# Scores and AV on 64-key partition halves, with the global outputs merged into AV

## The chip, the cores and the metric

One core of one Trainium2 chip. The metric is the device time in microseconds (us) of one execution. The engines are named as in the profile: PE (matmul), PEld (PE's weight loads, which overlap its matmuls), DVE (vector), ACT (activation), POOL and SP. Every run told here was in the fast state, except the one single-round run whose state is unknown, which is marked.

## The reference

Attention with a band of local keys and 32 global tokens, then a two-layer MLP with a quick GELU:

```python
batch, n_heads, seq_l, seq_g, head_dim = (8, 8, 512, 32, 64)
window = 32
k_all = concatenate([k_g, k_l]); v_all = concatenate([v_g, v_l])
out_g = softmax(scale * q_g @ k_all.T) @ v_all               # global queries see all keys
s_ll  = scale * q_l @ k_l.T, masked to |pos - pos'| <= window # local: band of 65 keys
s_lg  = scale * q_l @ k_g.T                                   # ... and the 32 global keys
out_l = softmax([s_lg, s_ll]) @ [v_g, v_l]
x = [out_g, out_l] as tokens x 512
h = x @ w_in                        # 512 -> 2048
g = h / (1 + exp(-1.702 * h))
out = g @ w_out                     # 2048 -> 512
```

## The kernel before

It works on head groups of four heads (two per batch element, 16 in all) and on MLP blocks of 512 tokens. While the MLP's second product of one block runs, the attention of the next block is fitted between its matmuls. All of these parts are matmuls on PE:

- `S`, the scores: transposed, keys on the output partitions. A round has two chunks of 128 keys; each chunk meets only the queries that its band touches. A 32-row part of PE holds one head, so four heads run at once on 32x128 tiles.
- `K` and `ekU`: scores of the global keys, and the opening of the three accumulators (sums and two halves of the output) with the global values.
- `U`, AV: adds exp(scores) times values, and times ones for the sums, into those accumulators; 128x32 tiles, four heads at once.
- `Gm`: the outputs of the global queries, 66 columns each.

```python
WIN = ((0, 10), (6, 12), (14, 12), (22, 10))      # per chunk: first query residue, how many
qt = consts.tile([128, 24, 32], F32)              # queries, with global queries before and after
...
def S(self, rnd, ...):
    for c in (2 * rnd, 2 * rnd + 1):
        ...
        for e in range(2):                        # the two halves of a head's dimension
            for j in range(4):                    # four heads, four 32-row tiles
                nc.tensor.matmul(ps[j][:, off : off + n],
                    lhsT=self.k[p, 128 * c : 128 * c + 128, e],
                    rhs=self.q[p, lo:hi, r0 : r0 + nr, e], ...)
...
def U(self, unit):                                # unit 0: sums, 1 and 2: output halves
    for c in range(4):
        ...
        for j in range(4):
            lv = (ones32 if unit == 0 else self.v[:, j, c, :D] ...)
            nc.tensor.matmul(ov[32 * j : 32 * j + 32, :] ... [:, :, r0 : r0 + nr],
                lhsT=lv, rhs=self.E[c // 2][:, j, at : at + 16 * nr],
                start=False, stop=(c == 3), ...)

def Gm(self, og=None):
    for c in range(5):                            # 4 key chunks and the global keys
        for j in range(4):
            ...
            nc.tensor.matmul(og[32 * j : 32 * j + 32, : D + 2], lhsT=lv, rhs=rv, ...)
...
def phase_o(i):                                   # second MLP product of block i
    ...                                           # with the attention of block i + 1
    o(0)                                          # o(t): 16 matmuls of 512 columns
    c.S(0)
    a.UG(c)                                       # ekUs, then U for three units, then Gm
    ...
    o(1)
    c.S(1)
    ...
    o(2)
    a2.S(0)
    c.UG(a2)
    ...
    o(3)
```

## Time and profile before

| kernel before | |
|---|---|
| time, median of 3 runs | 311.04 us (310.78 to 311.09) |
| span of the profiled run | 309.3 us |
| PE busy | 97% |
| steady period, one MLP block | 34.40 us (first MLP matmul of block 3 at 125.89, of block 4 at 160.29) |
| longest weight-load wait in AV that no semaphore explains | 0.4 us |

How to read it: the page's slices are fortieths of the span, each digit a busy share in tenths. PE is full everywhere, so the path that sets the end is PE itself, and an instruction or a pause added to PE is paid in full. The prediction shows these lines. One line of the waits view is added here, because the result turns on it. It gives the engine, the line that waited, what it waited for ("issue": nothing that the profile shows), then us in total, times, and the longest in us:

```profile
PEld L397 <- issue: 7.3, 20, 0.4
```

L397 is the matmul of `U`. Its weight loads paused 20 times with no semaphore to blame, never over 0.4 us: ordinary pauses while PE was busy with the matmuls ahead.

### The profile page before, as it was taken

To read this page: it belongs to the slowest core of one execution; us is meant where nothing else is said; L and a number is where in the kernel's file an instruction comes from. 1 tells how busy PE (TensorE), PEld (TensorE's weight loads), DVE (VectorE), ACT (ScalarE), POOL (GpSimd) and SP (SyncE) were. 2 spreads that over 40 slices of the span, in tenths; PEclk is the share of its full clock that TensorE was granted. 3 is DMA by queue.
4 is the path that set the end of the run, shared out by engine and by line. 5 is a ranking of instruction groups with operands and counts; after the bars stand their busy time and mean duration, and the time that the engine had idled before them with its cause. 6 is when DMAs were issued, how large, how long until landed. Compare 5 with 4: busy or idle time off the path is not lost.

```text
span 309.3 us, 7765 instructions
## 1 busy us (share of the span) xinstructions
PE 299.2 (97%) x3230; PEld 149.3 (48%) x3265; DVE 211.0 (68%) x446; ACT 167.6 (54%) x251; POOL 54.1 (18%) x86
## 2 busy tenths in 40 slices
PE   7899999999999999999999999999999999999994
PEld 6544445444454455444454455445454454446653
DVE  6668857978957876776867876776777855573320
ACT  4728475475546735565556645565456651673421
POOL 8542754630050001400050002100000000000000
PEclk9999999999999999999999999999999999999999
DMA  7999999999289013951199013901120012201122
GB/s 193 176 209 206 201 138 217 213 184 100 61 79 192 5 36 72 131 107 30 45 95 173 8 37 71 101 0 36 36 61 10 2 44 46 51 0 35 35 68 69
DMA packets 53859, 27.60 MB, mean 89 GB/s; under 512 B 42432, under 2 KB 43712, under 8 KB 53824
## 3 DMA queue, kind: packets, MB, share of 16 engines
q0 software_dynamic: 45696, 16.95, 48.2%
q1 hardware_dynamic: 7648, 9.51, 12.6%
q10 hardware_dynamic: 480, 0.66, 0.7%
q8 instruction: 25, 0.41, 0.6%
q14 instruction: 10, 0.08, 0.1%
HBM read 35.13 MB, written 8.91 MB: 142 GB/s over the span
## 4 chain that ended last, share of the span: by engine, by line
PE 88%; DVE 4%; ACT 2%; DMA 2%; issue 1%; POOL 1%; ACTq 0%; POOLq 0%
PE op L491 35%; PE hp L466 35%; PE s L297 6%; PE ov L397 4%; PE ov L374 3%; DMA rk<-in_k_l_dram 2%; ACT e L327 1%; DVE xL L430 1%; PE s L316 1%; PE op L503 1%; DVE gT L474 1%; PE s L466 1%; PE s L415 1%; ACT th L473 1%; PE kb L316 1%
## 5 line engine op out<-in xcount | busy, mean ns | idle before, releaser
L491 PE MATMUL op<-w_out_sb,gT 128*128 128x512 bf16 x504 | 120.0, 380 | 1.7 <-issue 0.5
L474 DVE SCALAR_TENSOR_TENSOR gT<-th,hp 128x512 bf16<-128x512 f32 (+1 forms) x140 | 91.1, 656 | 41.8 <-ACT th L473 40.5
L466 PE MATMUL hp<-xL,w_in_sb 128*128 128x512 bf16 x487 | 108.4, 379 | 0.7
L473 ACT ACTIVATE th<-hp 128x512 f32<-128x512 f32 (+1 forms) x140 | 79.8, 573 | 42.9 <-PE hp L466 39.4
L466 PEld LDWEIGHTS <-w_in_sb 128*128 128x128 bf16 x576 | 56.1, 98 | 65.0 <-issue 1.3
L491 PEld LDWEIGHTS <-gT 128*128 128x128 bf16 x528 | 49.3, 98 | 56.4 <-issue 3.5
L327 ACT ACTIVATE e<-s 128x1712 bf16<-128x1712 f32 x31 | 49.5, 1597 | 15.8 <-PE s L415 8.9
L505 ACT ACTIVATE ob<-op 128x512 f32<-128x512 f32 (+2 forms) x35 | 20.5, 585 | 60.3 <-PE op L491 57.7
L89 POOL DMA_DIRECT2D v<-in_v_l_dram x24 | 18.7, 786 | 115.9 <-PE s L415 111.0
L421 DVE STREAM_TRANSPOSE sT<-ov 128x512 f32<-128x512 f32 x15 | 10.8, 717 | 29.1 <-PE ov L397 29.1
L334 DVE TENSOR_TENSOR e<-e,mask 128x1408 bf16<-128x1408 bf16 x28 | 24.4, 871 | 6.5 <-ACT e L327 6.5
L297 PE MATMUL s<-q,kT 32*128 32x228 bf16 (+5 forms) x528 | 21.1, 280 | 0.9 <-DVE q L259 0.7
L430 DVE TENSOR_TENSOR xL<-ov,rs 128x512 bf16<-128x512 f32 x30 | 19.4, 686 | 1.8 <-PE ov L397 0.5
L297 PEld LDWEIGHTS <-kT 32*128 32x128 bf16 x528 | 11.1, 95 | 14.8 <-issue 9.4
L255 DVE STREAM_TRANSPOSE kT<-rk 128x512 f32<-128x512 f32 (+1 forms) x17 | 16.9, 993 | 1.4 <-DMA rk<-in_k_l_dram 1.3
L362 ACT ACTIVATE ek<-kb 128x512 bf16<-128x512 f32 x16 | 9.6, 601 | 9.5 <-PE kb L316 9.5
L397 PE MATMUL ov<-e,v 128*32 128x160 bf16 (+1 forms) x480 | 12.1, 239 | 0.0
L425 DVE STREAM_TRANSPOSE rs<-rT 128x512 f32<-128x512 f32 x16 | 11.4, 711 | 0.5
L259 DVE STREAM_TRANSPOSE q<-rq 128x512 f32<-128x512 f32 (+1 forms) x17 | 10.7, 634 | 0.0
L397 PEld LDWEIGHTS <-v 128*32 128x32 bf16 x512 | 10.0, 97 | 0.9 <-issue 0.9
L316 PE MATMUL kb<-q,kgT 32*32 32x512 bf16 x128 | 10.0, 386 | 0.0
L466 PE MATMUL hp<-xG,w_in_sb 128*128 128x256 bf16 x64 | 9.6, 273 | 0.1
(78 smaller groups left out, 165.9 us busy)
## 6 DMA issues: line engine op xcount, KB each, us to landing
out_dram<-ob SPq DMA_DIRECT2D x132, 64.0 KB, 1.7
v<-in_v_l_dram POOLq DMA_DIRECT2D x32, 128.0 KB, 6.5
rq<-in_q_l_dram POOLq DMA_DIRECT2D x6, 512.0 KB, 8.5
rk<-in_k_l_dram POOLq DMA_DIRECT2D x6, 512.0 KB, 10.4
w_out_sb<-in_moe_w_out_dram POOLq DMA_DIRECT2D x4, 512.0 KB, 11.3
w_in_sb<-in_moe_w_in_dram POOLq DMA_DIRECT2D x4, 256.0 KB, 10.2
w_in_sb<-in_moe_w_in_dram POOLq DMA_DIRECT2D x2, 512.0 KB, 12.5
rq<-in_q_l_dram POOLq DMA_DIRECT2D x3, 256.0 KB, 7.9
```

Of the source, the lines that this page charges most:

```text
L89: nc.gpsimd.dma_start(out=vtiles[b % 2][p, s, :, :, :D], in_=vf[b, g][:, hs])
L255: nc.vector.transpose(self.kT.rearrange("p (r t) -> p t r", t=16)[:, lo:hi], loaded[self.b][0][:, self.u].bitcast(F32)[:, 32 * lo : 32 * hi])
L297: nc.tensor.matmul(ps[j][:, off : off + n], lhsT=self.k[p, 128 * c : 128 * c + 128, e], rhs=self.q[p, lo:hi, r0 : r0 + nr, e], start=(e == ...
L327: nc.scalar.activation(e[:, :, :RW], self.ps[:, :, :RW], AF.Exp, scale=scale)
L334: nc.vector.tensor_mul(e, e, mask[:, rnd : rnd + 1, :].to_broadcast([128, 4, LW]))
L397: nc.tensor.matmul(ov[32 * j : 32 * j + 32, :].rearrange("p (t r) -> p t r", t=16)[:, :, r0 : r0 + nr], lhsT=lv, rhs=self.E[c // 2][:, j, ...
L430: nc.vector.tensor_mul(self.x[:, 2 * self.u + h, :], self.st[1 + h], self.st["rs"])
L466: nc.tensor.matmul(hp[:, : width(i)], lhsT=w_in_c[:, fc // 8, kc, fc % 8 // 2, :, fc % 2], rhs=(xL[i] if i < B else xG)[:, kc, :], start=( ...
L473: nc.scalar.activation(th[:, :n], hp[:, :n], AF.Tanh, scale=0.851)
L474: nc.vector.scalar_tensor_tensor(gTs[i][:, fc, :n], in0=th[:, :n], scalar=1.0, in1=hp[:, :n], op0=ALU.add, op1=ALU.mult)
L491: nc.tensor.matmul(op, lhsT=gTs[i][:, fc, tci * 128 : tci * 128 + 128], rhs=w_out_sb[:, fc, :], start=(first and fc == 4 * f4), stop=(fc = ...
L505: nc.scalar.activation(ob[:, lo:hi], op[:, lo:hi], AF.Copy, scale=0.5)
```

## The change

Its intent is to stream fewer columns. A half chunk of 64 keys with a band of 32 on each side meets 128 queries, so splitting the 128-key chunks trims what is computed outside the band; on 64x32 tiles the two halves run at the same time. The 66-column global outputs become a fourth unit beside the three of AV, so that every phase has two units, one on each row half. A PE drain (meant to hold the next matmuls back until those before it are done) is put between the second and the third phase, where the units change row halves, so that the two halves do not write one accumulator in the wrong order.

```diff
-    WIN = ((0, 10), (6, 12), (14, 12), (22, 10))
-        qt = consts.tile([128, 24, 32], F32, name="q%d" % i)
+        qt = consts.tile([128, 24, 36], F32, name="q%d" % i)
...
         def S(...)
-            for c in (2 * rnd, 2 * rnd + 1):
+            for ci in range(2):
+                c = 2 * rnd + ci
                 for e in range(2):
-                    for j in range(4):
-                        nc.tensor.matmul(ps[j][:, off : off + n],
-                            lhsT=self.k[p, 128 * c : 128 * c + 128, e],
-                            rhs=self.q[p, lo:hi, r0 : r0 + nr, e], ...)
+                    for h in range(2):
+                        r0 = 4 * (2 * c + h)
+                        for j in range(4):
+                            nc.tensor.matmul(ps[j][64 * h : 64 * h + 64, off : off + 8 * (hi - lo)],
+                                lhsT=self.k[p, k, e], rhs=self.q[p, lo:hi, r0 : r0 + 8, e], ...)
...
-        def U(self, unit): ...
-        def Gm(self, og=None): ...
+        def L(self, og=None):
+            for units in ((0, 2), (1, 3), (2, 0), (3, 1)):      # one unit per row half
+                if units == (2, 0):
+                    nc.tensor.drain()
+                for c in range(5 if 3 in units else 4):
+                    for j in range(4):
+                        for h, unit in enumerate(units):
+                            p = slice(64 * h, 64 * h + 64)
+                            ...
+                            else:
+                                nc.tensor.matmul(self.st[unit][o] ... [:, :, lo:hi], lhsT=lv,
+                                    rhs=e[:, 32 - 32 * h : 160 - 32 * h] ..., ...)
...
-    (prologue: a.U, c.B, c.S, a.Gm and the first MLP products interleaved; v_g by way of SP and a cast)
+    (prologue: all of a.L, then c's scores, then all of c.L, then the MLP; v_g straight to bf16 by POOL)
...
-            (last head group: units between output matmuls)
+            (last head group: ekUs and L, as everywhere)
```

The last two hunks are told in words; many lines are cut.

> **What bounds the kernel now.** I read the page first (engines, slices), then the groups of PE by shape, then the chain of waits, then the timeline of PE in one steady stretch. The page:
>
> ```profile
> span 309.3 us, 7765 instructions
> PE 299.2 (97%) x3230; PEld 149.3 (48%) x3265; DVE 211.0 (68%) x446; ACT 167.6 (54%) x251; POOL 54.1 (18%) x86
> PE   7899999999999999999999999999999999999994
> PEclk9999999999999999999999999999999999999999
> DMA  7999999999289013951199013901120012201122
> q8 instruction: 25, 0.41, 0.6%
> ```
>
> PE is busy in every slice at full clock. DVE (68%) and ACT (54%) have room; DMA is only dense in the first tenth. So the time is set by how many columns PE streams and by what it loses between matmuls. The chain agrees: PE carries 88% of it. A part of the chain in the steady state (start, duration):
>
> ```profile
> 116.35 3.56 PE op L491 x16
> 119.91 0.59 PE s L297 x16
> 121.30 1.03 PE ov L397 x48
> 122.49 0.32 PE op L491
> 122.87 3.19 PE op L491 x14
> 126.05 7.55 PE hp L466 x35
> ```
>
> The two MLP products cannot change: 35 matmuls of 512 columns in 7.55 us are 0.2157 us each, 0.421 ns a column. What changes is the attention between them. PE's timeline of one such piece (start, duration):
>
> ```profile
> 119.84 0.66 PE L297 MATMUL s<-q,kT 32*128 32x200 bf16 x16
> 120.44 0.20 PE L316 MATMUL s<-qgT,kgT 32*32 32x32 bf16 x4
> ...
> 120.92 0.38 PE L374 MATMUL ov<-ek,rvg 32*32 32x512 bf16 x4
> 121.23 0.49 PE L397 MATMUL ov<-e,ones 128*32 128x160 bf16 x16
> 121.55 0.78 PE L397 MATMUL ov<-e,v 128*32 128x160 bf16 x32
> 122.16 0.30 PE L415 MATMUL s<-v,e 128*32 128x66 bf16 x16
> 122.29 0.20 PE L415 MATMUL s<-rvg,eg 128*32 128x66 bf16 x4
> 122.42 1.04 PE L491 MATMUL op<-w_out_sb,gT 128*128 128x512 bf16 x3
> ```
>
> Start to next start (durations overlap, so they must not be summed): one scores round 0.60 us, AV with sums 0.93 (121.23 to 122.16), global outputs 0.26, both together 1.19. Per group of four concurrent matmuls a 66-column group takes 0.033 us (0.13 for four); but the last such group before the big matmuls takes 0.13. A change of tile shape therefore costs about 0.10 us.
>
> **What the Trainium skill says.** "TensorEngine Tiling (Array Packing)", Key Properties: changing the tiling mode drains the engine, different tiles run in parallel. The trace agrees: 0.10 us at each change. "TensorE: Matmul & The Clock Gate", Part 3: packed tiles overlap and weight loads are pulled ahead where row groups differ. The trace agrees: sixteen score matmuls of 200 to 228 columns fit in 0.60 us. "Advanced Engine Details and Errata", SBUF Cachelines: 16-byte lines, a penalty where accesses do not reuse a line. Scores read q with a 4-byte step in runs of 10 or 12; 10 from a line start touch 3 lines of 4 (12 places), 12 from place 6 touch 4 lines (16). Rounded up, a round has 2 x (20 x 12 + 19 x 16) = 1088 columns, 0.458 us, against 856 or 0.360 unrounded; measured 0.60 - 0.10 = 0.50. The rounded count fits. "Runtime: NRT & Kernel Launch", Instruction fetch mechanics: blocks of 16 KiB, 256 instructions, two lines. The q8 row (25 packets, 0.41 MB) fits PE's 6495 instructions; whether fetching ever stalls is not visible here.
>
> **The change part by part.** Same tile-mode changes per head group (four heads); 16 head groups, two scores rounds each.
>
> Scores: 128-key tiles (32x128) become 64-key halves (32x64), eight concurrent tiles of 160 columns; per round 4 groups as before. The new q tile starts every run of 8 at a multiple of 4 and is padded by 2, so a run is exactly two lines. Per round 4 x 160 x 0.421 = 0.269, plus 0.004 a group (what AV shows over its columns: 12 groups of 2112 columns, 0.889, took 0.93) = 0.285, plus the mode change 0.10 = 0.39. It was 0.60. I take 0.205 saved; x 32 = -6.6 us. All lie on the bound engine.
>
> AV: before 12 groups of 160 or 192 columns plus 5 of 66, 1.19 us with the change out. After: four phases, each with two units concurrently on 64-row halves (8 tiles of 64x32), 4 groups of 128 columns each: 16 x (0.054 + 0.004) = 0.93, plus two extra groups of 66 columns, 0.07, plus the change out 0.10, together 1.10. So the global outputs ride for free and would save 0.09. But the drain in the middle: the next group then starts after the last one has left (a 66-column matmul lasts 0.195) instead of 0.033 later, +0.16, plus a restart of the emptied queue which I guess at 0.07. So 1.10 + 0.23 = 1.33, +0.14 a head group; x 16 = +2.2 us.
>
> Last head group: it now has the ordinary order. Before it alternated modes three times: 256.66 to 260.15 in the chain less four big matmuls (0.86) = 2.63 us. After: 0.75 (ek products and a change) + 1.33 = 2.08. That is -0.55, against the +0.14 counted: -0.7 us.
>
> Exp and mask: exp goes from 1712 to 1280 columns (1597 ns x 1280/1712, about 1.2 us), the mask multiply from 1408 to 1280. ACT and DVE are not the bound: 0 in the steady state. The separate small exp for gE is there already in 15 of 16 cases.
>
> Prologue (to about 23 us): the second head group's q extension no longer follows its k transpose, so its first scores could start up to 0.7 us earlier than 12.20. Against it: two converting loads of v_g now precede v and w_in on the POOL queue; v of the first head group landed 12.4 us in a full DMA and is needed at about 12.7, so it may be late by 0.5 to 1; the second group's ek products now write the banks that its exp still reads (about 1 us of PE idle at 16 to 17); and the sums (unit 0) end in the third of four phases instead of the first, so the 1/sum chain (0.73 + 0.27 + 0.71 + 0.69 us) starts later where little covers it. Net guess +0.5.
>
> Instruction supply: per head group PE's load-matmul pairs go from 32 to 64 in scores and from 68 to 132 in AV, 96 pairs or 192 instructions more. The dense stretch of scores, global, ek and AV has some 380 instructions in 2.5 us, so a block of 256 can be used up in under 2 us while its successor is fetched. Guess +0.6 in all.
>
> Sum: -6.6 + 2.2 - 0.7 + 0.5 + 0.6 = -4.0; 311.0 - 4.0 = 307.0 us.
>
> **Rivals.**
> 1. Issue becomes the bound. AV asks for eight load-matmul pairs in 0.058 us, 7 ns a pair. The timeline shows bursts of 3 to 4 ns a pair from a full queue, but never more than a few dozen in a row, and the longest sustained rate is 8 ns (four pairs in 0.033, where the columns bind anyway). At 10 ns a pair AV takes +0.35 a head group (+5.6 us) and scores +0.01 a group of eight (+1.7): 313 to 315 us. For it: instruction count of PE rises by half. Against: no sign yet of a limit.
> 2. The drain costs little or is hidden and fetching never stalls: AV at 1.15 us, and the gain is the full scores saving plus the end: 303.5 to 304.5 us, over 2%.
> 3. The two row halves of a column tile do not run at full rate together (different PSUM banks, same partitions). Then AV nearly doubles, +0.9 x 16 = +14 us, 320 us or more. Against it: the old scores already have four row groups writing four banks of all partitions at line rate.
> 4. DVE comes onto the path: sums end about 0.65 us later in AV, and the chain sum, scale, mask, transposes leads to the next scores. In the trace DVE finishes these about 1.5 us before they are needed; with shorter mask and fewer copies 0.9 remains. I expect 0; at worst +0.3 per stage, 2 us.
>
> **Range and chances.** The scores saving is the surest (read from start-to-start times), the drain +-0.1 us x 16, issue and fetch 0 to +6, prologue -0.5 to +1.2. So 307.0, with 303.5 to 311.0 for 8 in 10. Two per cent would be 304.8: chance of faster 0.2 (rival 2), within 2% 0.72, slower 0.08 (rivals 1 and 3 together).
>
> **What would show it.** In the changed trace: scores round start to next start 0.39 (right) or 0.45 and more (issue or unaligned reads). AV without the drain 0.5 us per half; groups of eight at 0.058; the gap at the drain 0.2 to 0.3 us. PE still over 95% busy with no waits of the score matmuls for DVE. A period of the steady state (one 512-token block, 34.4 us before) of 33.9. At the start the first MLP matmul of block 0 at about 19 to 20 us and its 17th at 23.5 to 24. If gaps inside groups appear that no semaphore explains, at every 256 instructions, the fetch term is larger than I put it; if the period is above 34.4, rival 1 or 3 holds and the prediction is wrong.

## The result, and the profile after

| | before | after |
|---|---|---|
| time, median | 311.06 us (310.78 to 311.22, 4 runs) | 328.31 us (327.10 to 329.19, 4 runs) |
| ratio | | 1.0553 (95%: 1.0510 to 1.0595) |
| span of the profiled run | 309.3 us | 325.2 us |
| first MLP matmul | 19.31 us | 27.74 us |
| first matmul of the second MLP product | 33.66 us | 43.00 us |

A ratio here is the mean time of one kernel's fast runs over that of the other's of the same rounds, so not quite the ratio of the medians. The changed kernel is correct and slower by 5.5%; 307.0 had been predicted.

The page of the changed kernel:

```profile
span 325.2 us, 10817 instructions
PE 299.5 (92%) x4759; PEld 149.5 (46%) x4801; DVE 207.7 (64%) x416; ACT 154.3 (47%) x250; POOL 55.3 (17%) x88
PE   7647999799999998999999989899999989999995
PEclk9978999999999999999999999999999999999999
q8 instruction: 37, 0.61, 0.8%
```

PE's busy time is the same as before (299.5 against 299.2), so the 15.9 us of span are not more busy time but pauses (the profiled run is the fastest of the four; by the medians 17.3 us were lost). The share fell from 97% to 92%, most in slices 2 to 4, some spread over the rest, and the clock fell in slices 3 and 4. Instruction packets rose from 25 to 37: PE has 9560 recorded instructions instead of 6495, and the 3065 more are 12 blocks of 256 but for 7.

The chain of waits of the changed kernel in the stretch that the prediction showed of before (start, duration, what):

```profile
120.84 0.43 PE s L286 x31
...
122.07 0.37 PE ov L409 x27
...
122.84 0.40 PE ov L409 x26
...
123.39 0.77 issue
...
124.50 0.32 PE op L481
...
124.88 3.18 PE op L481 x14
```

The scores round (L286) shrank to 0.43 us. AV (L409) begins at 122.07 with full speed, pauses at the drain until 122.84, and then stands still in its second half until 124.16, with "issue" as the reason: PE waited for nothing that the profile shows. PE's weight loads at that place (start, duration, what; in brackets the idle time before and its reason) stop at the same moment: no instruction of either kind starts.

```profile
122.52 0.09 PEld L397 LDWEIGHTS <-eg 64*32 64x32 bf16 x1
122.83 0.09 PEld L409 LDWEIGHTS <-v 64*32 64x32 bf16 x1 [0.23 <-issue]
...
123.16 0.09 PEld L409 LDWEIGHTS <-v 64*32 64x32 bf16 x1
124.16 0.09 PEld L401 LDWEIGHTS <-e 64*32 64x32 bf16 x1 [0.90 <-issue]
```

The first pair is the drain: about 0.3 us between the last weight load before it and the first after it. The second is the stop, 1.00 us in the middle of a group.

The waits view of the changed kernel:

```profile
PEld L409 <- issue: 15.3, 37, 1.9
PE s L401 <- issue: 3.9, 4, 1.3
PE kb L304 <- issue: 3.3, 1, 3.3
```

Where the longest pause of AV's weight loads was 0.4 us, it is 1.9, and one pause of 3.3 us lies in the K matmuls (L304). That one is in the prologue. PE's timeline there (start, duration, instruction, count, idle time before):

```profile
17.07 0.68 PE L304 MATMUL kb<-q,kgT 32*32 32x512 bf16 x6
21.01 0.61 PE L304 MATMUL kb<-q,kgT 32*32 32x512 bf16 x2 [3.26 <-issue]
21.54 0.76 PE L286 MATMUL s<-q,kT 32*64 32x160 bf16 x32
23.66 0.61 PE L363 MATMUL s<-ek,ones 32*32 32x512 bf16 x4 [1.36 <-ACT e L317]
24.04 1.09 PE L363 MATMUL s<-ek,rvg 32*32 32x512 bf16 x8
```

Eight matmuls with equal operands that are all ready, and PE stops after six of them. Afterwards it is slow too: the 32 score matmuls take 0.76 us here and 0.50 in the steady state. The Trainium skill, "TensorE: Matmul & The Clock Gate", Part 1, says that the clock falls to half after about 3.4 us of idleness. The trace agrees for this pause: PE had just idled for 3.26 us by the profile's ends, 3.67 counted from the last start, and the granted clock is 0.5 from 20.48 to 27.31 us. In two runs below a shorter pause was enough. With the AV matmuls halved, the clock was 0.5 from 55.14 to 58.55, after a pause of 2.73; with 128 instructions inserted, from 59.95 to 63.37, after one of 1.67. In the 3.41 us just before these three falls PE was busy for 0.68, 0.88 and 1.40 us.

Where the 15.9 us of span are, from start to start of the same matmuls in both traces:

| stretch | before | after | difference |
|---|---|---|---|
| start to the first matmul of the second MLP product | 33.66 | 43.00 | +9.3 |
| from there to the MLP of block 1 | 22.02 | 23.98 | +2.0 |
| from there to a scores round in the second product of block 2 (105.39 and 116.78) | 49.71 | 49.80 | +0.1 |
| four steady periods, from there | 137.6 | 141.7 | +4.1 |
| the rest | 66.3 | 66.7 | +0.4 |

The pauses that no semaphore explains, counted from start to start, make up most of it: 1.91 us at 13.10, 3.67 at 17.33, 0.58 at 26.29, 1.19 at 57.92, then 0.99 at 123.16, 0.80 at 134.36, 1.37 at 193.61, 1.14 at 205.18 and 1.49 at 264.74. The sum is 13.1 us.

### The profile page after: what moved, and what is told of

Same layout as the page of the kernel before. It is cut to its first block, busy times and chain, and to the rows that moved or that the text cites. A ratio compares the mean times of both kernels' runs of the same rounds, so it can differ in the third digit from the quotient of the medians.

```text
span 325.2 us, 10817 instructions
## 1 busy us (share of the span) xinstructions
PE 299.5 (92%) x4759; PEld 149.5 (46%) x4801; DVE 207.7 (64%) x416; ACT 154.3 (47%) x250; POOL 55.3 (17%) x88
## 4 chain that ended last, share of the span: by engine, by line
PE 83%; DMA 8%; issue 4%; DVE 3%; ACT 1%; POOL 0%; ACTq 0%
PE hp L456 35%; PE op L481 34%; DMA rk<-in_k_l_dram 6%; PE ov L409 5%; PE s L286 4%; DMA w_in_sb<-in_moe_w_in_dram 2%; PE ov L363 2%; PE kb L304 1%; PE op L493 1%; DVE xL L425 1%; PE s L304 1%; PE s L401 0%; DVE sT L416 0%; DVE rs L420 0%; DVE gT L464 0%
## 5 line engine op out<-in xcount | busy, mean ns | idle before, releaser
L456 PE MATMUL hp<-xL,w_in_sb 128*128 128x512 bf16 x502 | 112.2, 379 | 2.1 <-DMA rk<-in_k_l_dram 0.8
L317 ACT ACTIVATE e<-s 128x1280 bf16<-128x1280 f32 x31 | 38.3, 1235 | 23.2 <-PE s L397 9.1
L323 DVE TENSOR_TENSOR e<-e,mask 128x1280 bf16<-128x1280 bf16 x28 | 22.5, 803 | 7.8 <-ACT e L317 7.8
L409 PE MATMUL ov<-e,v 64*32 64x128 bf16 (+1 forms) x896 | 21.5, 218 | 3.4 <-issue 1.7
L409 PEld LDWEIGHTS <-v 64*32 64x32 bf16 x1024 | 18.7, 93 | 8.7 <-issue 8.7
L401 PE MATMUL s<-v,e 64*32 64x66 bf16 x448 | 13.1, 199 | 4.4 <-issue 3.9
L286 PE MATMUL s<-q,kT 32*64 32x160 bf16 (+2 forms) x1056 | 16.6, 239 | 0.5 <-DVE q L249 0.5
L286 PEld LDWEIGHTS <-kT 32*64 32x64 bf16 x1056 | 10.3, 105 | 13.9 <-issue 8.9
L304 PE MATMUL kb<-q,kgT 32*32 32x512 bf16 x128 | 11.5, 418 | 3.7 <-issue 3.3
L401 PEld LDWEIGHTS <-e 64*32 64x32 bf16 x512 | 11.9, 90 | 5.2 <-issue 4.5
L409 PE MATMUL ov<-e,ones 64*32 64x128 bf16 (+1 forms) x448 | 11.4, 215 | 1.7 <-issue 1.7
```

What stands on the lines that cost most here:

```text
L286: nc.tensor.matmul(ps[j][64 * h : 64 * h + 64, off : off + 8 * (hi - lo)], lhsT=self.k[p, k, e], rhs=self.q[p, lo:hi, r0 : r0 + 8, e], sta ...
L317: nc.scalar.activation(e, self.ps[:, :, :RW], AF.Exp, scale=scale)
L323: nc.vector.tensor_mul(e, e, mask.rearrange("p (o w) -> p o w", o=1).to_broadcast([128, 8, KW]))
L401: nc.tensor.matmul(og[o], lhsT=e[:, 128 * h : 128 * h + 32], rhs=self.v[p, j, c, :], start=(h == 1 and c == 0), stop=False, skip_group_che ...
L409: nc.tensor.matmul(self.st[unit][o].rearrange("p (t r) -> p t r", t=16)[:, :, lo:hi], lhsT=lv, rhs=e[:, 32 - 32 * h : 160 - 32 * h].rearra ...
L456: nc.tensor.matmul(hp[:, : width(i)], lhsT=w_in_c[:, fc // 8, kc, fc % 8 // 2, :, fc % 2], rhs=(xL[i] if i < B else xG)[:, kc, :], start=( ...
```

## The experiments

Theory: PE runs out of instructions. The stretch of scores, global keys, `ekU` and AV has, counted from the program, 384 PE instructions without a 512-column MLP matmul among them (64 + 16 + 16 + 24 + 264), where before it had 224 (32 + 16 + 16 + 24 + 136). In a stretch without a stop it runs from 156.81 to 159.56, 7.2 ns an instruction. If a block of 256 comes more slowly than that, and the stretch holds a whole block, PE has to stop. Rivals: AV on row halves is slow by itself (columns, banks, issue pace); the drain; the accumulators or the DVE chain; in the prologue the reordered loads.

### More instructions, same columns, in the kernel before

Every AV matmul of the kernel before was cut into two column halves; nothing else was touched.

```diff
-            for c in range(4):
+            for c, half in ((c, half) for c in range(4) for half in range(2)):
...
-                        ov[32 * j : 32 * j + 32, :] ... [:, :, r0 : r0 + nr],
-                        lhsT=lv, rhs=self.E[c // 2][:, j, at : at + 16 * nr],
+                        ov[32 * j : 32 * j + 32, :] ... [:, 8 * half : 8 * half + 8, r0 : r0 + nr],
+                        lhsT=lv, rhs=self.E[c // 2][:, j, at + 8 * nr * half : at + 8 * nr * half + 8 * nr],
```

> The kernel before, with every AV and sum matmul cut into two of half the columns: same columns, same tile shapes, same waits, no drain; only PE's instructions rise (96 per head group in AV, about 1540 in all). Instruction-supply theory (PE runs out of instructions when it eats a block of 256 in less than about 3 us): gaps of 0.3 to 1.5 us that no semaphore explains appear in the dense stretches, and the time rises to 315 to 320 us. Rival (the changed kernel is slow because of 64-row tiles, the drain, or the order of its prologue, none of which is here): at most 1 us of issue cost, 311 to 312 us.

Measured: 321.73 us median (320.96 to 321.95), before on the same chip 310.83; ratio 1.0327 (1.0279 to 1.0375). Correct. The waits view of this kernel:

```profile
PEld L397 <- issue: 14.4, 24, 2.7
PE ov L397 <- issue: 5.9, 3, 2.5
```

L397 is the same line of `U` as in the kernel before: its longest pause went from 0.4 to 2.7 us. The six pauses over 0.7 us add up to 9.4 of the 10.9 us lost (1.51 at 14.51, 2.28 at 19.76, 2.73 at 52.35, 0.85 at 60.35, 1.34 at 130.29, 0.71 at 191.55). There are no row halves here, no drain, no merged unit and no new order of loads. More instructions alone make PE stop, somewhat more than expected.

### Half the AV instructions, same columns, in the changed kernel

AV takes two chunks of 256 columns instead of four of 128. The result is wrong on purpose (relative error 1.03); the order, the waits, the drain and the columns of units 0 to 2 are those of the changed kernel (the global unit has half its matmuls, beside the others).

```diff
-                for c in range(5 if 3 in units else 4):
+                for c in ((0, 2, 4) if 3 in units else (0, 2)):
...
-                                    rhs=e[:, 32 - 32 * h : 160 - 32 * h] ...,
+                                    rhs=self.E[c // 2][p, j, 32 - 32 * h : 288 - 32 * h] ...,
```

> The changed kernel with half the AV instructions for the same PE columns: two key chunks instead of four, each with 256 columns instead of 128 (wrong result on purpose). Tile shapes, drain, order and DMA as in the changed kernel. Instruction-supply theory: the unexplained gaps in AV go almost wholly, the steady block takes about 34.4 us in each case, the first output product of block 0 starts near 35 us instead of 43.0, total 310 to 316 us. Rival (tile shapes, drain, order of the prologue): nothing changes, 326 to 329 us.

Measured: 315.42 us median (313.75 to 316.75), before 310.83; ratio 1.0126 (1.0067 to 1.0185). So 13 of the 17 us come back when AV has half its instructions. In its trace the chain of waits has no piece of "issue" over 0.15 us from 57 to 290 us, and the unexplained pauses fall from 13.1 to 2.9 us. Some 3 us more come of a shorter AV: 1.33 us a head group, where the changed kernel takes 1.52 without a stop. That is also why the steady period, 34.06 us, is 0.34 below that of before. It is not a gain of the change as it stands, whose periods without a stop take 34.44. The row halves, the drain and the DVE chain, all still there, are refuted as the cause of the large loss. The issue pace of AV is changed here together with the count, and the next two experiments tell these apart. What is left over lies in the start: the first MLP matmul of block 0 is at 21.74 us, 2.4 later than before, with 0.71 and 1.08 us of unexplained pauses (a third, of 1.14, is at 52.70), 1.39 us of waiting for the exp and 1.21 us of waiting for the scaled outputs. The first output product of block 0 is at 37.22 us, where near 35 had been expected. That part is read from its trace only.

### Where the stops fall: 128 instructions more

If the stops come at block boundaries, they depend on how many instructions went before. 64 tiny pairs of weight load and matmul were put into the MLP of block 2 of the changed kernel, half a block of 256.

```diff
+                if i == 2 and fc == 7:
+                    bp = pbank("shift")
+                    for n in range(64):
+                        j = n % 4
+                        nc.tensor.matmul(bp[32 * j : 32 * j + 32, 0:32], lhsT=warm[32 * j : 32 * j + 32, 0:32],
+                                         rhs=warm[32 * j : 32 * j + 32, 0:32], start=True, stop=True, ...)
```

> The changed kernel with 64 tiny load-matmul pairs (128 instructions, half a block of 256; about 0.5 to 0.7 us of PE time) in the MLP of block 2, before the steady blocks. The steady period holds about 4.5 blocks of instructions, so stalls fall in every second period. Instruction-supply theory: from there on the gaps move to the other periods: those near 191, 203 and 263 us vanish and gaps appear in the stages near 157 to 167 and 228 to 238 us; total within 2 us of the changed kernel. Rival (gaps belong to the work, DMA traffic or clock of these stages): they stay in the same stages.

Measured: 327.06 us median (326.34 and 327.78); ratio 1.0503 (1.0425 to 1.058). Its chain of waits has these pieces of "issue" over 0.2 us between 100 and 250 us:

```profile
159.15 1.27 issue
...
170.85 1.18 issue
...
230.70 1.01 issue
...
242.08 0.65 issue
```

In the changed kernel such pieces begin at 123.39, 134.56, 193.81 and 205.41. With half a block inserted they are gone from there and stand in the periods between. After 250 us it has none, where the changed kernel had one at 264.94. The work at 123 and at 159 is the same, one period apart, so neither the operands nor a bank nor the drain can be what stops PE; the position in the instruction stream is.

The traces show the position to the instruction. Count a weight load with its matmul as two, and PE's drains and semaphore instructions as one each. Then the nine stops of the changed kernel come after 450, 705, 962, 1729, 4033, 4545, 6337, 6849 and 8641 instructions, and each of these numbers leaves 193 or 194 over a multiple of 256. So do the eight stops of this run (the last four after 5314, 5826, 7618 and 8130), the six with the AV matmuls halved, the three with half the AV instructions, and the five of the burst below.

The counts fit: a period of the changed kernel has 1152 PE instructions, 4.5 blocks, so a stretch that holds a whole block in one period does not in the next. The changed kernel's periods alternate accordingly: 36.04, 34.44, 36.76, 34.46 us. From one dense stretch to the other within a period there are 512 instructions, two blocks, which is why the stops come in pairs. The kernel before has 768 a period, 3 blocks, and 224 in the stretch, less than a block.

### How fast instructions come: a burst by itself

768 tiny pairs, 1536 instructions, in the MLP of block 4 of the kernel before, with nothing to wait for.

```diff
+                if i == 4 and fc == 7:
+                    bp = pbank("burst")
+                    for n in range(768):
+                        (the matmul of the experiment above)
```

> The kernel before with 768 tiny load-matmul pairs (1536 instructions, 6 blocks of 256) in the middle of the MLP of block 4, where DMA is nearly idle and nothing is waited for. Instruction-supply theory: the pairs run at about 8 ns until the supplied instructions are used up, then stop at every 256 instructions until the next block has come; the spacing of the stops is the time to fetch a block, about 3 us, so the burst takes 14 to 18 us and the kernel 325 to 329 us. Rival (supply is no limit, only issue at 8.3 ns a pair): 6.4 us without stops, the kernel 317 to 318 us.

Measured: one run, 335.59 us, its state unknown, with a granted clock of 0.964 against 0.998 of before. PE's timeline:

```profile
174.67 1.22 PE L764 MATMUL burst<-warm 32*32 32x32 bf16 x128 [4.38 <-issue]
178.13 1.22 PE L764 MATMUL burst<-warm 32*32 32x32 bf16 x128 [2.23 <-issue]
181.58 1.22 PE L764 MATMUL burst<-warm 32*32 32x32 bf16 x128 [2.23 <-issue]
185.03 1.23 PE L764 MATMUL burst<-warm 32*32 32x32 bf16 x128 [2.23 <-issue]
190.15 2.34 PE L466 MATMUL hp<-xL,w_in_sb 128*128 128x512 bf16 x5 [0.22 <-issue]
```

Exactly 128 pairs, 256 instructions, run in about 1.2 us; then PE waits 2.2 us, so that each 256 begin 3.45 us after the 256 before them began. So the supply in a straight line of code is 256 / 3.45 us, 13.5 ns an instruction, and it comes in blocks. That is half of what the dense stretch of the changed kernel asks for (7.2 ns) and also slower than the old stretch (224 in 2.58 us, 11.5 ns), which gets by because it is shorter than a block. The instruction packets of this trace show where the time goes: PE goes on at 178.12, the next packet begins only at 179.26 and takes until 180.18, and PE starts on the next block at 181.58. The three parts are 1.14, 0.92 and 1.40 us. The Trainium skill, "Runtime: NRT & Kernel Launch", Instruction fetch mechanics, has the blocks of 256 and a prefetch in a straight line, and the trace agrees; its sentence that crossing a block is "mostly hidden" does not hold here. The burst cost more than expected because of its first stop (4.38 us) and because the clock fell once more (0.5 from 173.81 to 194.29): the five 512-column matmuls of the last line take 2.34 us, 0.43 us between starts, twice the usual 0.216.

In the changed kernel the same is seen from the other side. The trace's instruction packet of 121.90 to 122.85 us is followed by PE's restart at 124.16, that of 132.94 to 133.82 by 135.16, that of 18.73 to 19.68 by 21.01: 1.31, 1.34 and 1.33 us after the packet's end, also in the prologue's long stop. Over all nine stops it is 1.29 to 1.58 us.

### Spreading the instructions out

To leave time for a fetch, eight 512-column output matmuls were put between the second and third phase of AV in the changed kernel; the drain stayed.

```diff
-                    nc.tensor.drain()
+                    if between:
+                        between()
+                    nc.tensor.drain()
...
-        a.UG(c)
-        c.XK()
+        a.UG(c, lambda: o(1, (0, 1)))
...
-        o(1)
+        o(1, (2, 3))
```

> The changed kernel with eight big output matmuls (1.73 us of PE work from 32 instructions) put between the second and third phase of AV in the steady stages, drain kept. Same work, more tile-mode changes (about 0.2 us for each of 11 head groups, +2.2 us). Instruction-supply theory: the stretch is less dense, the steady gaps of 0.6 to 1.3 us go (together about 5 us), total 323 to 326 us, prologue as before the edit. Rival (the array itself is slower): only the mode changes show, 329 to 331 us.

Measured: 336.89 us median (335.32 to 337.29); ratio 1.0808 (1.0743 to 1.0874). A miss. The stops in the steady state went, as the theory says, but a new wait came, in the waits view of this kernel:

```profile
PE s L286 <- DVE xg L435: 9.7, 6, 1.6
```

The next scores need the bank that holds the global outputs, and it comes free only when the last DVE step of the chain after AV has read it. With half of the 16 output matmuls moved ahead of AV's end, the other half does not cover that chain. The period became 36.9 us. The order of work before and after AV was not free to change without moving that accumulator.

### The loads of the prologue

The load of v_g was put back to where the kernel before has it, with the cast after it.

```diff
-    load_turned(nc.gpsimd, rvg[:, 0:2, :D], vgf[:, 0:2, :])
+    load_g32("v", vgf)
...
+    cast_g32("v", rvg)
```

> The changed kernel with the load of v_g for the first two head groups put back as it was (plain loads on the SP queue and a cast on DVE), so v and w_in are issued as early as before. Rival for the prologue (its 9.3 us are lost to the order of the loads): first output product of block 0 clearly earlier than 43.0 us, total under 325 us. Instruction-supply theory: gaps at the same count of instructions, total 326.5 to 329.5 us.

Measured: 329.28 us median (328.27 to 329.6); ratio 1.0587 (1.057 to 1.0604). The first matmul of the second MLP product is at 42.72 us against 43.00, and the pauses stand where they were (1.50 us at 13.28, 3.68 at 17.11, 1.48 at 57.6). The place of this load is not what costs 9 us in the prologue.

### The aligned reads alone, in the kernel before

The prediction had put part of the old scores round down to reads of q that start in the middle of a 16-byte line. Only the tile of q was padded, and everything in it moved by 2; the instructions are the same in number and columns.

```diff
-        qt = consts.tile([128, 24, 32], F32, name="q%d" % i)
+        qt = consts.tile([128, 24, 36], F32, name="q%d" % i)
...
-            self.q = self.qt.bitcast(BF16).rearrange("p t (r e) -> p t r e", e=2)
+            self.q = self.qt.bitcast(BF16).rearrange("p t (r e) -> p t r e", e=2)[:, :, 2:34]
...
-            nc.vector.transpose(self.qt[:, 4 + lo : 4 + hi, :].rearrange("p t r -> p (t r)"),
+            nc.vector.transpose(self.qt[:, 4 + lo : 4 + hi, 2:34],
...
-                    self.qt[:, t0 : t0 + n, r0 : r0 + nr],
+                    self.qt[:, t0 : t0 + n, 2 + r0 : 2 + r0 + nr],
```

> The kernel before with one thing of the change alone: the q tile padded by two places at each side, so that three of the four score windows start on a 16-byte line. Rounded up to whole lines a scores round streams 936 columns instead of 1088, 152 fewer, 0.064 us; 32 rounds, -2.0 us. The k_g product reads rows that now start off a line (up to +0.03 us a group), but it ran beside the ek products in the changed kernel without lengthening them. Line theory: a scores round goes from 0.595 to 0.53 us start to next start, total 308.7 to 309.5 us. Rival (the 0.14 us above the plain column count is weight loading or issue): rounds stay at 0.595, total 311 to 312 us.

Measured: 309.05 us median (308.88 to 310.03, 6 runs), before 310.90 (11 runs); ratio 0.9946 (0.9933 to 0.996). Correct. PE's timeline of this kernel in the same piece as before:

```profile
119.05 0.60 PE L297 MATMUL s<-q,kT 32*128 32x200 bf16 x16
119.58 0.21 PE L316 MATMUL s<-qgT,kgT 32*32 32x32 bf16 x5
```

From start to next start the round takes 0.53 us instead of 0.60. So the explanation by lines holds, for this term. (The edit also makes a row of q 36 places long instead of 32; that this alone does nothing was not tested.) This version beats both kernels: 0.54% below the kernel before, which is under the 2% that would count as faster, and 5.9% below the changed one by the medians.

### All runs

| run | median us | ratio to before | unexplained pauses |
|---|---|---|---|
| changed kernel | 328.31 | 1.0553 | 13.1 us |
| before, AV matmuls halved | 321.73 | 1.0327 | 9.4 us |
| changed, half the AV instructions | 315.42 | 1.0126 | 2.9 us, all before 54 us |
| changed, 128 instructions inserted | 327.06 | 1.0503 | moved by a period |
| before, burst of 1536 | 335.59 (one run) | | 3.45 us per 256 instructions |
| changed, AV spread out | 336.89 | 1.0808 | steady ones gone, new wait |
| changed, old load of v_g | 329.28 | 1.0587 | as in the changed kernel |
| before, q aligned | 309.05 | 0.9946 | none in AV over 0.5 us |

What could not be tried: the changed kernel without its drain. Two tiles on different row halves would then write the same accumulator with nothing in the program to order them, so a time measured so would not be that of a correct kernel. What the drain costs is therefore read from the trace alone.

## Why the prediction was wrong

**The step that failed: "Instruction supply", "Guess +0.6 in all".** The prediction had the right mechanism and nearly the right count ("some 380 instructions in 2.5 us"), even the reason why a block could be used up early, and then put a guess in place of a size. The term measured 13.1 us of stops. The missing number was the time that a block takes to come: 3.45 us, against 1.8 us in which the dense stretch uses one up (256 x 7.2 ns), so by this reckoning up to 1.6 us are lost each time a whole block falls into a stretch (0.80 to 1.49 in the steady state; in the prologue a stop lasts up to 3.67). The profile of before could not show it, since its stretches are shorter than a block. The insertion of half a block shows that it is this, and the halved matmuls in the old kernel show that it needs nothing else of the change.

**The prologue, "Net guess +0.5".** It measured +9.3. Two stops of 1.91 and 3.67 us and a small one of 0.58 are 6.2 of it. The wait of the `ek` products for the exp, put at "about 1 us", was 1.36. The late sums it also foresaw: after its first seven matmuls the MLP stands still from 29.04 to 30.26, until DVE has scaled the outputs (that step ends at 30.21; the profile names a load there), where the kernel before waited 0.58 us. What is left is put down, from the trace only, to the halved clock after the long stop, which the prediction did not have: the twelve `ek` products take 1.40 us to the start of AV (23.66 to 25.06), where they take 0.76 in the steady state with K's matmuls beside them (157.28 to 158.04). "v of the first head group ... may be late" is not needed to explain anything.

**AV, 1.33 us.** Without a stop it measured 1.52 (158.04 to 159.56), so +0.33 a head group and not +0.14. Two terms were too small. The pace: a group of eight pairs takes 0.067 us, not 0.058, that is 8.3 ns a pair; only the first groups, already queued, go faster. Rival 1 was therefore half right, with a much smaller effect than its 10 ns a pair. And the drain costs about 0.32 us from the last start to the next, where 0.23 in addition to the 0.03 of an ordinary step had been put. Times 16, AV gives 5.3 us away.

**Scores, 0.39 us.** Measured 0.43 from 120.77 to 121.20: each step of eight tiles had been put at 0.071, and the first takes 0.10, the next two 0.073 to 0.08. The saving is 0.165 x 32 = 5.3 us, not 6.6. It equals what AV lost, which is why the periods without a stop, 34.44 and 34.46 us, are within 0.1 of the 34.40 of before and not at the 33.9 predicted. So even with no stop the change would have brought nothing in the steady state in this form.

**What held.** The reason of the old round's length (the aligned version shows it). The second head group's first scores start 0.7 us earlier (11.49). Exp and mask shorter, 1597 to 1235 and 871 to 803 ns, and off the path. The last head group went from 2.63 to 2.28 us, a gain of 0.35 where 0.55 had been put. Rival 3 (row halves do not run together) is refuted: a group of eight takes 0.067 us, where the 128 columns of each half one after the other would need 0.108. Rival 4 (DVE on the path) is refuted in the steady state, where no score matmul waits for DVE; it became true only when AV was spread out.

**A misreading.** "DMA is only dense in the first tenth" is wrong: the page shows it at 90% or more in slices 2 to 10, so for a quarter of the span. No term of the sum rests on it.

**The chances.** "Slower" had 0.08, from rivals 1 and 3 alone; the fetch was in the range only with "0 to +6". The sentence that gaps inside groups would mean that "the fetch term is larger than I put it" is what came true.

**What stays open.** Why the stop at 17.33 lasts 3.67 us where the steady ones last 0.8 to 1.5; its packet took 0.95 us, like others, but began at 18.73, 1.4 us after PE had run dry. The first stop of the burst (4.38 us) is alike: its packet began at 172.41, 2.3 us after the last start, with DMA nearly idle. What delays these packets is not shown. What the drain costs without the rest. And how the 13 us would split between prologue and steady state in another order of the prologue.

## What to carry to other kernels

Count the instructions of each dense stretch on PE, weight loads included, and not only its columns: halving a tile's rows doubles the count for the same columns, and once a stretch holds a whole fetch block that is used up faster than the next one comes (3.45 us for 256 here), PE stops. The sign of it is a pause of PE and of its weight loads together, in the middle of a group, with "issue" as the reason, which moves when instructions are inserted elsewhere and comes at the same count of instructions modulo 256. Before splitting tiles for fewer columns, look for a gain with the same instructions, as the padded q gave here.

## What the Trainium skill lacked or had wrong

- "Runtime: NRT & Kernel Launch", Instruction fetch mechanics: it calls the cost of crossing a block "mostly hidden" behind a slow issue. Here small load and matmul pairs went at 8.3 ns a pair, a block of 256 came every 3.45 us (13.5 ns an instruction), and the changed kernel lost 13.1 us to it. The page has no time for a block; packets of 16 KB took 0.9 to 1.8 us, and the changed kernel's PE resumed 1.3 to 1.6 us after a packet's end.
- "TensorE: Matmul & The Clock Gate": Part 1 says that start-to-start "never drops below ≈25 ns however small N is", and Part 3 puts the issue overhead of packed tiles at about 4 ns a tile. Here pairs of a weight load and a matmul that take turns on different tiles kept to 8.3 ns a pair (eight in 0.067 us), between the two. No page found has a sustained pace for such pairs on packed tiles.
- No page found has the cost of an explicit PE drain between groups of matmuls: about 0.32 us from start to next start here.
- "Advanced Engine Details and Errata", SBUF Cachelines: it does not say what a partly used line costs PE. Counting every line touched as used in full gives a difference of 0.064 us between the two rounds; measured were 0.60 us as it was and 0.53 us with the starts on lines.
